# Gated delta attention and a two-layer MLP on one core: chunk 2's normalised rows turned by VectorE and transfers instead of TensorE, with a new order of steps

## The chip, the cores and the metric

The kernel runs on one core of one Trainium2 chip. The metric is device time in microseconds (us); lower is better. TensorE is called PE, VectorE DVE, ScalarE ACT, GpSimd POOL and the engine that issues most transfers SP, as in the profile.

## What is computed

A delta-rule attention runs over 768 positions for 4 batches of 8 heads of width 48, and its output, 768 rows of 384 numbers per batch, goes through a block with layer norm, two matrix products and a residual:

```python
k_n = k / (np.linalg.norm(k, axis=-1, keepdims=True) + 1e-06)
for t in range(S):
    y[:, :, t] = np.einsum('bhd,bhde->bhe', q[:, :, t], state)
    v_old = np.einsum('bhde,bhd->bhe', state, kt)
    state = state + bt[:, :, :, None] * np.einsum('bhd,bhe->bhde', kt, vt - v_old)
...
x = y.transpose(0, 2, 1, 3).reshape(B, S, H * D)
xn = (x - mu) / np.sqrt(var + 1e-06) * g_ln
return x + np.maximum(xn @ w_ch1, 0.0) @ w_ch2
```

All numbers are float32. `w_ch1` is 384 x 1536, `w_ch2` 1536 x 384.

## The kernel before

The 768 positions are cut into 12 chunks of 64 (`C`, `NCH`). A chunk holds the 64 positions of all 32 pairs of batch and head, and gives 256 rows of x (`TOK`), in two groups of 128 (`g`). For each chunk the kernel does the following.

- Keys and queries are brought in with the head's width on the partitions (`first_kt` by PE transposes in the first chunks, `turned`, L753, by DVE from blocks that transfers laid out). `gram` (L790) multiplies keys by keys, `queries` (L799) queries by keys; both run on PE at L775.
- The triangular system of a chunk is inverted. Chunk 0 does it on PE, DVE and ACT in rounds of products called E and Z (`first_inverse`, L648; products at L722 and L741, DVE at L687 and L731, ACT at L681). From chunk 1 on, 32-row blocks are inverted row by row on DVE (`rows_inverse`, L826; L860 and L867), two chunks at a time from chunk 2 on: blocks come by eight transfers `gb` (L833), results go through DRAM (`xd`, L871) and come back by transfers `xt` (L873). `join` (L883) makes 64-row inverses of the blocks: a DVE transpose L888, 64 small matmuls L898, ACT L910, 64 small matmuls L904, ACT L916.
- `recur` (L971) carries the state: products of keys and of queries with the state (L983), the solution u (L1017, copied by ACT at L1019), the state's update (L1034, added by DVE at L1044), and y (L1024). Chunk 0 has its own u (L1000, DVE L1005).
- ACT evicts y as x (L1062) and makes the layer norm (`ln_act`, L939 to L969; DVE takes a reciprocal at L967).
- The normalised rows have to be turned, so that the 384 columns lie on the partitions (`xnt`). Up to chunk `LNPE` PE does this: three 128x128 transposes per group (L1096), each evicted by ACT with the factor g_ln (L1111). Above `LNPE`, DVE turns 32x32 blocks (L1073, two instructions), one transfer writes them to DRAM (`xld`, L1078), four read them back into place (`xnt`, L1082), and ACT multiplies by g_ln (three instructions, L1088).
- The MLP: chunk 0 in halves (`by_halves`, L1317; L1326 and L1341 on PE), chunks 1 to 3 with plain first products (L1300, 12 groups of 6 matmuls; ACT evicts them with ReLU at L1309), and chunks from `FROM` = 4 on with 15 products for the first layer (`fifteen`, L1172; L1221 on PE, sums on DVE at L1241, ACT at L1237 and L1243, differences on POOL at L1197). The second layer of chunks 1 on takes 7 products where a plain one takes 8 (`seven`, L1402; PE at L1423, differences on POOL at L1410 and L1449, sums on DVE and POOL at L1441). Rows that come by the way through DRAM stand in another order within the chunk; L1177 and L1310 put that right in the access patterns, which read `LNPE`.

The weights are fetched as 32-bit words and converted by ACT, DVE and POOL (`fetch`, `convert`, L507 to L544) while chunks 0 and 1 run.

The code first records every piece of work as a numbered step with its engine, without emitting it (`Line.add`). The text `ORDER` (L59 to L156) lists the step numbers, and `Line.emit` (L187) emits them in that order; `in_this_order` (L26) then keeps each engine, and the queues of transfers, to it. So `ORDER` is the order in each engine's queue. An entry `z` emits a fill, a matmul whose result nobody reads (`zeros`, L1514); other fills are steps (`fill`, L553). Each engine takes its instructions strictly in order: one that waits holds up all behind it. POOL and ACT also issue transfers from their own queues.

PSUM has eight banks: `two` and `by` (two each) serve the attention, `f0` to `f3` mostly the MLP. The turn of chunk 2 uses `by`:

```python
for g in range(2) if c <= LNPE else ():
    tp, bk = (by[:, g], BY[2 * g : 2 * g + 2]) if c else ((two, by)[g][:, 0], (TWO, BY)[g][0:2])
```

Of the kernel before, what the change touches and what calls it, by code (L numbers as in the profile page):

```python
# [63 lines left out]
155 243 148 238 151 236 332 152 225 675 156 z 215 157 240 159 158 214 237 239 160 216 162 161 257 46 241 168 164 166 333 206 165 334 245 207 417 163  # L64
# [136 lines left out]
def kernel(  # L201
# [21 lines left out]
    GH = 2 * H  # L223
    NP = H // 2
    TURNED = 4
    LNPE = 2
    GP = 2 * NP
    FROM, LATER = 4, 6
    TOK = 256
# [1423 lines left out]
```

## Time and profile before

| | |
|---|---|
| time, median of 3 runs | 510.0 us (508.62 to 510.16) |
| time of the profiled execution | 510.58 us |
| its span, first to last instruction | 508.8 us |
| granted PE clock, mean over the span | 0.965 |
| busy: PE, DVE, ACT, POOL | 488.6, 353.8, 249.0, 275.6 us |
| PE turns L1096, all chunks (18 instructions) | 2.2 + 0.9 us |
| DVE turns L1073 (18 instructions) | 10.0 us, 565 ns each |
| ACT L1111 (12 + 3) and L1088 (27) | 3.5 + 0.9 and 12.5 us |
| transfers `xld`, `xnt`: median from issue to landing | 3.3 and 3.2 us |

A span is the time between the first and the last instruction on the core; the device time has some 1.8 us around it. A busy time counts an engine's own instructions. A matmul's weights are loaded by a separate instruction (PEld) that overlaps with PE. In the groups, "out<-in" are the program's names. The clock is the share of full speed that PE was granted: in the first 56 us it changes between 0.5 and 1, then it stays at 1 until the end.

### The profile page before, as it was taken

To read this page: it belongs to the slowest core of one execution; us is meant where nothing else is said; L and a number is where in the kernel's file an instruction comes from. 1 tells how busy PE (TensorE), PEld (TensorE's weight loads), DVE (VectorE), ACT (ScalarE), POOL (GpSimd) and SP (SyncE) were. 2 spreads that over 40 slices of the span, in tenths; PEclk is the share of its full clock that TensorE was granted. 3 is DMA by queue.
4 is the path that set the end of the run, shared out by engine and by line. 5 is a ranking of instruction groups with operands and counts; after the bars stand their busy time and mean duration, and the time that the engine had idled before them with its cause. 6 is when DMAs were issued, how large, how long until landed. Compare 5 with 4: busy or idle time off the path is not lost.

```text
span 508.8 us, 22190 instructions
## 1 busy us (share of the span) xinstructions
PE 488.6 (96%) x9606; PEld 447.6 (88%) x9606; DVE 353.8 (70%) x780; ACT 249.0 (49%) x620; POOL 275.6 (54%) x430
## 2 busy tenths in 40 slices
PE   7778999999899999999999999999999999999996
PEld 3667988788788898899999999999999999999996
DVE  9668987997679648896649898568899328143251
ACT  5758873643544524627435535435563257363230
POOL 5464537264755496438894363492543850645633
PEclk9756799999999999999999999999999999999999
DMA  8988796667656566546834434766154402211101
GB/s 168 293 160 190 249 200 85 98 152 130 90 86 87 187 119 119 65 99 149 194 58 62 94 62 135 150 94 97 50 92 106 111 20 45 60 48 46 24 18 31
DMA packets 196097, 54.99 MB, mean 108 GB/s; under 512 B 186076, under 2 KB 189404, under 8 KB 196000
## 3 DMA queue, kind: packets, MB, share of 16 engines
q1 hardware_dynamic: 189920, 40.58, 41.9%
q10 hardware_dynamic: 3872, 9.83, 6.0%
q0 software_dynamic: 2208, 3.17, 3.8%
q8 instruction: 75, 1.23, 1.0%
q14 instruction: 22, 0.18, 0.1%
HBM read 36.64 MB, written 16.91 MB: 105 GB/s over the span
## 4 chain that ended last, share of the span: by engine, by line
PE 90%; DVE 5%; issue 2%; POOL 1%; DMA 1%; SPq 0%; ACT 0%; DVEq 0%; POOLq 0%; ACTq 0%
PE f L1423 29%; PE f L1221 22%; PE f L1300 9%; PE f L1326 4%; PE f L1341 3%; PE by L983 2%; PE by L1024 2%; PE two L983 2%; PE by L775 2%; PE two L1017 2%; PE two L775 2%; PE two L1034 2%; PE f L775 1%; DMA xt<-xd 1%; PE by L741 1%
## 5 line engine op out<-in xcount | busy, mean ns | idle before, releaser
L1410 POOL TENSOR_TENSOR h_all<-h_all 128x256 f32<-128x256 f32 x123 | 89.9, 742 | 135.1 <-PE f L1423 121.3
L1423 PE MATMUL f<-w_sb,h_all 128*128 128x192 f32 x492 | 109.8, 332 | 1.6 <-DVE rstd L967 1.6
L1423 PEld LDWEIGHTS f<-w_sb,h_all 128*128 128x128 f32 x492 | 81.8, 190 | 3.6 <-issue 1.9
L1423 PE MATMUL f<-words,h_all 128*128 128x192 f32 x396 | 84.5, 330 | 0.3 <-POOL h_all L1410 0.3
L860 DVE TENSOR_TENSOR tmp<-xb,gb 128x87 f32<-128x87 f32 (+21 forms) x186 | 73.7, 396 | 4.9
L867 DVE TENSOR_TENSOR xb<-xb,tmp 128x87 f32<-128x87 f32 (+21 forms) x186 | 73.6, 396 | 4.8
L1241 DVE TENSOR_TENSOR h_all<-h_all,f 128x512 f32<-128x512 f32 x96 | 63.5, 682 | 14.3 <-PE f L1221 13.2
L1423 PEld LDWEIGHTS f<-words,h_all 128*128 128x128 f32 x396 | 66.6, 190 | 1.7 <-POOL h_all L1410 1.0
L1300 PE MATMUL f<-xnt,w_sb 128*128 128x256 f32 x216 | 50.2, 382 | 0.0
L349 POOL DMA_DIRECT2D tb<-in_k_dram x64 | 42.0, 660 | 10.3 <-DVE kt L755 9.4
L1243 ACT ACTIVATE h_all<-h_all 128x512 f32<-128x512 f32 x48 | 28.5, 624 | 34.6 <-DVE h_all L1241 34.3
L1300 PEld LDWEIGHTS f<-xnt,w_sb 128*128 128x128 f32 x216 | 40.2, 190 | 5.3
L1237 ACT COPY h_all<-f 128x512 f32<-128x512 f32 x48 | 26.2, 590 | 34.3 <-PE f L1221 17.4
L1441 DVE TENSOR_TENSOR o<-f,x 128x192 f32<-128x192 f32 x33 | 11.6, 352 | 38.9 <-PE f L1423 22.3
L1221 PE MATMUL f<-words,w_sb 128*128 128x128 f32 x256 | 31.7, 276 | 0.0
L1309 ACT ACTIVATE h_all<-f 128x256 f32<-128x256 f32 x36 | 13.3, 382 | 35.1 <-PE f L1300 34.9
L1221 PEld LDWEIGHTS f<-words,w_sb 128*128 128x128 f32 x256 | 30.0, 192 | 0.2
L1221 PE MATMUL f<-xnt,w_sb 128*128 128x128 f32 x192 | 25.4, 276 | 0.0
L542 POOL TENSOR_TENSOR w_sb<-words 128x768 uint32<-128x768 uint32 (+1 forms) x11 | 15.0, 1365 | 17.7 <-DVE words L529 13.3
L1221 PEld LDWEIGHTS f<-xnt,w_sb 128*128 128x128 f32 x192 | 23.7, 192 | 0.1
L1326 PEld LDWEIGHTS f<-xnt,w_sb 128*128 128x128 f32 x144 | 19.2, 200 | 3.3 <-issue 0.2
L1088 ACT ACTIVATE xnt<-xnt,g_sb 128x256 f32<-128x256 f32 x27 | 12.5, 498 | 19.2 <-DMA xnt<-xld 19.1
(246 smaller groups left out, 958.4 us busy)
## 6 DMA issues: line engine op xcount, KB each, us to landing
words<-in_moe_w_ch_dram ACTq DMA_DIRECT2D x10, 768.0 KB, 5.2
gd<-gsb SPq DMA_DIRECT2D x11, 512.0 KB, 3.6
v<-in_v_dram SPq DMA_DIRECT2D x24, 192.0 KB, 4.3
kr<-in_k_dram SPq DMA_DIRECT2D x46, 96.0 KB, 3.6
out_dram<-o SPq DMA_DIRECT2D x44, 96.0 KB, 2.8
xld<-xlt SPq DMA_DIRECT2D x9, 384.0 KB, 3.3
xnt<-xld SPq DMA_DIRECT2D x36, 96.0 KB, 3.2
gb<-gd SPq DMA_DIRECT2D x44, 64.0 KB, 3.0
```

Of the source, the lines that this page charges most:

```text
L349: add(eng, cost, lambda: QUEUE[eng].dma_start(out=out_, in_=in_), r, w, bulk=n * ns / 16e3, **kw)
L775: nc.tensor.matmul(pair[hp][half(e ^ (hp & n)), (g * NP + j) * C : (g * NP + j + 1) * C], kt[drows(hp), l], rt[drows(hp), i],)
L860: lambda j=j, n=n, w=w, t=t: nc.vector.tensor_tensor(out=t, in0=xv[:, 0:n, j : j + 1].to_broadcast([np_, n, w]), in1=gv[:, j : j + 1, j + ...
L867: "DVE", dve(n * w), lambda t=t, rest=rest: nc.vector.tensor_tensor(out=rest, in0=rest, in1=t, op=ALU.subtract),
L1221: nc.tensor.matmul(wide(p[:, 128 * n : 128 * n + 128]), w[n // 2][:, n % 2 * 128 : n % 2 * 128 + 128], r, start=start and n == 0, stop=Tru ...
L1237: add("ACT", act(512), lambda: nc.scalar.copy(o, p), pk, ok)
L1241: add("DVE", dve(512), lambda: nc.vector.tensor_tensor(out=o, in0=o, in1=p, op=op), pk, ok)
L1243: add("ACT", act(512), lambda: nc.scalar.activation(o, o, ACTF.Relu), [], ok)
L1300: nc.tensor.matmul(p[:, 0:TOK], w1_sb[:, t, f * 128 : (f + 1) * 128], xnt[:, t], start=(t == 0), stop=(t == KC - 1))
L1326: nc.tensor.matmul(p[:, 0:128], w1_sb[:, t, f * 128 : (f + 1) * 128], xnt[:, t, cols], start=(t == 0), stop=(t == KC - 1))
L1410: add(eng, cost, lambda: e.tensor_tensor(out=out_, in0=x, in1=y, op=op), r, w, port=2 if eng == "Pool" else 1, pr=-2)
L1423: lambda f=f, t=start and f == 0: nc.tensor.matmul(p[:, 0:D2], lhs(f), rhs[:, f], start=t, stop=(f == F2 - 1), skip_group_check=True),
```

## The change

`LNPE` goes from 2 to 1, so that chunk 2 takes the way of chunks 3 on. Eight steps of chunk 2 (two PE turns of three transposes each, six ACT evictions) give way to ten (two DVE transposes, one transfer to DRAM, four back, three ACT products); all later steps are renumbered by two. `ORDER` is written anew over its whole length, for all engines, with two entries `z` in place of one. Nothing else is changed.

```diff
 ORDER = """
-1 9 49 50 8 63 52 51 10 5 250 54 71 11 56 0 6 14 7 12 47 62 53 48 23 13 72 55 36 18 64 42 26 37 61 27 58 60 77 81 15 28 17 32 331 43 73 88 29 40 65 79
...
 """
@@
     TURNED = 4
-    LNPE = 2
+    LNPE = 1
     GP = 2 * NP
```

The numbers of `ORDER` are left out above but for its first line before. The new order, in the program's names, as far as the steps below speak of it:

- Fills: one of the two stands after an L775 of chunk 0's inverse rounds, ahead of an L741; the other after chunk 0's first L1024, ahead of a gram L775 of chunk 2. Before, the one `z` stands after the first L722.
- ACT's first L426 and L596 stand ahead of L439, so that the built program holds two loads of an activation table in place of one, the second ahead of the first L596. POOL's memset L1539 stands behind the start.
- On DVE, chunk 0's L1005 stands behind an L731 that it was ahead of.
- Between chunk 2's L1024 and chunk 3's L898, PE has three pairs of L1423, where it had 12 pairs, the L1034 and the six turns.
- Between chunk 2's L1024 and chunk 2's first L1300, PE has 29 pairs of L1423, L898, L904, L1034, two L983, L775 and L1017.
- The `xld` transfer of chunk 2 and its four `xnt` stand next to each other on SP, with nothing between.

More of the change, by code (lines that the diff above doesn't have):

```diff
@@ L59 @@
 ORDER = """
[4 rows of a table removed]
-155 243 148 238 151 236 332 152 225 675 156 z 215 157 240 159 158 214 237 239 160 216 162 161 257 46 241 168 164 166 333 206 165 334 245 207 417 163
[88 rows of a table removed]
[3 rows of a table added]
+132 57 139 131 204 z 140 213 38 134 129 133 251 223 135 144 137 222 675 136 205 148 252 67 141 235 256 250 142 208 254 143 242 146 253 150 39 145 206
[3 rows of a table added]
+275 190 191 276 384 247 194 277 249 337 195 382 356 200 278 391 232 359 z 202 338 383 203 279 387 385 339 361 363 201 280 679 389 281 282 396 364 357
[85 rows of a table added]
 """
```

182 rows, old and new, of the table ORDER are left out of this document.

## The prediction

> **What bounds the kernel now.** I read the page first, then busy time by stretch, then the chain of waits in order of time, then the timeline around the places that the change touches. The page has TensorE (PE) nearly always at work and on nine tenths of the chain that ended last:
>
> ```profile
> PE 488.6 (96%) x9606; PEld 447.6 (88%) x9606; DVE 353.8 (70%) x780; ACT 249.0 (49%) x620; POOL 275.6 (54%) x430
> PE 90%; DVE 5%; issue 2%; POOL 1%; DMA 1%; SPq 0%; ACT 0%; DVEq 0%; POOLq 0%; ACTq 0%
> ```
>
> The stretches say where PE is not at work (first busy figure after the length):
>
> ```profile
> 0.00:20.00 20.00, 14.10 (x259) 9.31 (x260) 16.35 (x49) 12.09 (x29) 7.50 (x19) 0.89 0.97 219
> 20.00:40.00 20.00, 14.43 (x439) 12.53 (x441) 12.17 (x35) 12.79 (x33) 12.98 (x19) 0.59 0.82 186
> 120.00:140.00 20.00, 18.28 (x349) 16.28 (x342) 11.88 (x23) 9.70 (x30) 13.95 (x21) 1.00 0.74 98
> 140.00:160.00 20.00, 19.19 (x511) 16.73 (x512) 17.09 (x37) 7.44 (x21) 12.99 (x21) 1.00 0.44 74
> 160.00:480.00 320.00, 320.00 (x6285) 304.63 (x6284) 213.12 (x447) 153.86 (x375) 180.27 (x292) 1.00 0.46 92
> ```
>
> So there are three regimes. Up to about 55 us chunk 0's inverse is a chain of short PE, DVE and ACT steps, at a granted clock of 0.59 in the second row. Between 120 and 160 PE idles 1.72 + 0.81 = 2.53 us. From 160 to 480 it idles not at all: there a new order can win only by less PE work, and it can lose by any wait. Around the edit the chain (start, duration) reads
>
> ```profile
> 30.98 1.15 PE f L1515 x2
> ...
> 78.80 1.08 PE two L983 x64
> 79.87 0.93 PE by L983 x64
> ...
> 102.06 0.65 PE by L1096 x6
> ...
> 120.23 0.52 PE f L1423 x2
> ...
> 123.35 0.34 PE f L1423 x2
> ...
> 141.60 0.81 PE by L1096 x6
> ...
> 143.02 0.81 issue
> ...
> 150.92 2.59 PE f L1300 x12
> ```
>
> and the timeline (start, duration, engine, line; idle before in brackets)
>
> ```profile
> 2.25 1.28 ACT L439 ACT_TABLE_LOAD   x1 [2.25 <-issue]
> ...
> 134.87 0.49 ACT L1062 ACTIVATE x<-by 128x384 f32<-128x384 f32 x1 [1.78 <-PE by L1024]
> 135.79 0.71 DVE L888 STREAM_TRANSPOSE xnj<-xt 128x512 f32<-128x512 f32 x1 [2.63 <-DMA xt<-xd]
> 139.81 1.17 ACT L969 ACTIVATE xln<-xln,rstd 128x384 f32<-128x384 f32 x2 [0.98 <-DVE rstd L967]
> 139.85 0.89 PE L1423 MATMUL f<-w_sb,h_all 128*128 128x192 f32 x4 [1.60 <-DVE rstd L967]
> ...
> 216.66 1.03 DVE L1073 STREAM_TRANSPOSE xlt<-xln 128x384 f32<-128x384 f32 x2
> 222.12 3.48 SPq L349 DMA_DIRECT2D xnt<-xld  x4
> 227.93 1.31 ACT L1088 ACTIVATE xnt<-xnt,g_sb 128x256 f32<-128x256 f32 x3 [7.28 <-DMA xnt<-xld]
> ```
>
> Chunk 2's six turns are at 141.60; its first L1300 runs at 150.92, so nothing waited for them. PE's 1.60 us at 139.85 is DVE's doing: DVE stood 2.63 us at L888 for chunk 3's xt transfers, and the sums L1441 that free PE's banks stood behind it. The 0.81 us "issue" gap at 143.02, like those in the first 37 us (1.10, 1.60, 0.85 and 1.53 us), falls on every 256th PE instruction: an instruction fetch, which the change does not alter.
>
> **The change part by part.** All is summed against the profiled execution: span 508.8 us, its own time 510.58, that is 1.8 us around the span and 0.6 above the median of 510.0. I add the sum to the median.
>
> *Turns taken from PE.* Six L1096 go: 0.65 us where they follow other full-size matmuls (102.06), so −0.65. The ACT work falls from six L1111 (371 ns) to three L1088 (498 ns), 0.7 us on an engine 49% busy: nothing.
>
> *Changes of kind on PE.* A group of 64 small matmuls costs 1.08 us behind a full-size one and 0.93 behind another small group (78.80, 79.87); a full-size pair costs 0.52 behind a small group and 0.34 otherwise (120.23, 123.35). One excursion to small groups and back thus costs 0.15 + 0.18 = 0.33 us. Counted in both orders from chunk 1's L983 on, there are 64 such excursions before and 62 after: −0.7 (0 to −1.4, as two more are saved earlier, at half clock and among waits).
>
> *The new way of chunk 2's x.* Two L1073 (0.565 us each) join DVE, one xld and four xnt transfers SP. SP stands idle from 136.3 to 141.7 us, and in the new order nothing stands between these five: free for others. But the way is longer. From L1062 (134.87) to the end of L969 (140.98) it is 6.1 us, 0.98 of it a wait for DVE; from chunk 4's rows, L1073 at 216.66 to the end of L1088 at 229.24, another 12.6 (the xnt transfers issue 4.4 us after xld, and L1088 starts 5.8 after that). Together 17.7 to 18.7. In the new order PE has, between chunk 2's L1024 and its first L1300: 29 pairs of L1423 (0.325 each, 9.4), L898 and L904 (0.68 each), L1034 (0.86), L983 twice (1.08 each), L775 and L1017 (0.93 each) and three returns (0.19 each), together 16.3. So L1300 waits 1.4 to 2.4 us, and all of PE behind it. I take +1.9 (0 if PE is late there for another reason).
>
> *PE's wait for DVE at 139.85.* In the new order chunk 3's xt transfers stand some two SP issues (0.6 us each) further forward, but between chunk 2's L1024 and chunk 3's L898 PE has 9 L1423 pairs, the L1034 and the six turns fewer (2.9 + 0.86 + 0.81 = 4.6 us), and L888 still blocks DVE ahead of the sums. Between 0 and −1.6; I take −0.6, as the wait is likely met in another place.
>
> *The start.* The program now has two fills (L1515) where it had one. The row is 1.15 us; the second stands after chunk 0's first L1024, ahead of a gram that needs two L573 copies (0.58 each) held behind an L681, so part of it covers a wait: 0 to +1.15, taken +0.6. DVE's L1005 now stands behind an L731 whose product comes after L1000 on PE, not before it: +0.67 + 0.43, less the 0.83 of the last L741, now done ahead: +0.3. And the dummy square root L439, which loaded the square-root table at 2.25 us while ACT waited for data, is moved behind L596, so that the built program has a second table load just ahead of the first L596. POOL's memset L1539 (0.97 us at 2.19, during which DVE's L395 took 1.47 us in place of 0.18) is moved back as well. DVE is then up to 1.2 us sooner with L595, but the load starts only after the second square (about 7.9 us) and takes 1.28, so L596 comes at about 9.2, where it was (9.23). I take 0 (−1.2 to +1.3).
>
> The Trainium skill (ScalarE: Activation LUTs, What ACT_TABLE_LOAD costs) adds a drain of about 1.38 us to each load of another table set. The one load of the trace shows none (the next ACTIVATE starts 1.30 us after it), but nothing was ahead of it; by the page the sum would be 1.4 higher, an estimate.
>
> *160 to 480 us.* No idle to win. If the new order waits as much there as the old one does from 120 to 160, it loses 2.5; if it is as dense, 0. Margins between a PE product and the next use of its bank look alike in both orders; I take +1.0.
>
> Sum: −0.65 − 0.7 + 1.9 − 0.6 + 0.6 + 0.3 + 0 + 1.0 = +1.85, so 511.9 us: a small loss.
>
> **The rivals.** *Faster: the waits that the old order has are gone and the new one is hidden.* If PE comes to L1300 later than its data (any wait of 1.9 us behind L1024, for example at L898 for xt, does that), the term +1.9 falls; if the 1.6 us at 139.85 go wholly and the long stretch stays dense, what is left is −0.65 − 0.7 − 1.6 + 0.9 = −2.05: 507.9. For it: five SP issues and L1073 stand where both queues are free. Against: the way from L1024 has no slack worked out above. It decides once L1300 of chunk 2 waits under 0.5 us.
>
> *Faster: the clock rises one window earlier.* The granted clock changes at 42.8, 46.2 and 56.4, in steps of 3.41 us, and is 0.50 from 46.2 to 56.4 although PE is busy 3.40 of 3.40 us from 49.6 to 53.0, mostly with the small L775. A full-size fill in that window may lift the clock at 53.0. Six L1326 took 1.62 us at half clock and 0.67 later; 3.4 us of such work would take 1.6 to 2.0 less: 511.9 − 1.8 = 510.1, no change. The Trainium skill (TensorE: Matmul & The Clock Gate, What's actually happening) has the clock doubled after one busy window of about 3.4 us; the row from 49.6 to 53.0 does not agree, unless small matmuls count less.
>
> *Slower by more: the first 55 us stretch.* The chain there alternates engines, so one step out of place on DVE is met in full. Five rounds of E and Z products in two halves: if each half-round waits for one DVE L687 or L731 more (0.4 us), it is 10 × 0.4 = 4.0 on top: 515.9. For it: the new order puts a fill between L775 and the next L741 (1.15) and lets half 1 overtake half 0. Against: DVE's work ahead of L1005 is the same but for one L529 (0.35).
>
> *The change does not do what it says:* excluded; L1096 of chunk 2 is gone from the program.
>
> **How the numbers follow.** What a measurement here tells from no change is about 0.3%, 1.5 us. Forecast (+0.5 to +4, its own range 510.5 to 514): 0.42. Waits gone (about 507.9, down to 505.5): 0.28. Clock lifted (about 510.1): 0.16. Long start (about 515.9): 0.14. Faster by over 0.3% takes the second and a little of the third, 0.30; within 0.3% takes most of the third and the lower part of the forecast, 0.21; slower the rest, 0.49. The range leaves out a tenth on each side: below, some of the second case (506.3); above, half of the fourth (516).
>
> **What would show it.** Right: an idle of 1.4 to 2.4 us on PE before chunk 2's first L1300, released by ACT L1088; no L1096 after 110 us; a second ACT_TABLE_LOAD at about 8 us; two L1515 groups; L1326 starting 0.5 to 1.5 us after 54.46. Wrong: L1300 of chunk 2 without a wait, or idle time on PE between 160 and 480 beyond 2.5 us, or a start that differs by more than 2 us either way, since that is the part with the least support.

## The result, and the profile after

| | before | after |
|---|---|---|
| median (lowest to highest of 5 runs) | 509.5 us (507.28 to 510.16) | 515.51 us (514.48 to 516.58) |
| ratio to before, 95% interval | | 1.0141 [1.0111, 1.0171] |
| profiled execution, span | 510.58, 508.8 us | 515.51, 513.3 us |
| PE busy, and idle in the span | 488.55, 20.3 us | 488.2, 25.1 us |

The new order is slower by 7.2 us by the ratio (1.0141 of 508.7); the two profiled executions, which the rest of this section compares, differ by 4.9. The forecast was 511.9, a loss of 1.9: the sign and the range held, the size did not. 0.1% is 0.5 us in all that follows.

The first part of the page of the new kernel (busy time, share, instructions) and its shares of the chain that ended last:

```profile
PE 488.2 (95%) x9602; PEld 446.6 (87%) x9602; DVE 348.7 (68%) x782; ACT 249.3 (49%) x618; POOL 274.5 (53%) x430
PE 82%; DVE 5%; ACT 4%; DMA 3%; issue 2%; SPq 2%; POOL 1%; ACTq 0%; POOLq 0%; DVEq 0%
```

PE does as much as before; the whole difference of the spans is time in which it stands. The chain now has 5% of transfers and SP's queue, and PE 8% less of it. The stretches say where (first busy figure after the length is PE's, clock third from the end):

```profile
0.00:20.00 20.00, 13.39 (x260) 9.12 (x261) 13.25 (x50) 13.09 (x29) 6.97 (x21) 0.90 0.94 210
20.00:40.00 20.00, 15.06 (x462) 12.77 (x460) 13.44 (x36) 14.30 (x36) 13.36 (x16) 0.68 1.01 214
40.00:60.00 20.00, 15.65 (x438) 13.71 (x439) 16.69 (x47) 14.38 (x32) 9.34 (x10) 0.66 0.88 222
60.00:80.00 20.00, 18.40 (x244) 15.92 (x243) 14.46 (x39) 13.37 (x37) 10.21 (x11) 1.00 0.72 170
100.00:120.00 20.00, 18.74 (x323) 15.04 (x322) 18.72 (x46) 8.40 (x25) 7.73 (x12) 1.00 0.67 154
140.00:160.00 20.00, 18.65 (x480) 17.21 (x482) 16.52 (x33) 7.36 (x20) 9.58 (x15) 0.91 0.42 81
160.00:480.00 320.00, 319.04 (x6181) 302.05 (x6172) 213.72 (x449) 153.15 (x375) 177.88 (x289) 1.00 0.47 95
```

Idle time of PE, before and after: 13.1 and 15.9 us up to 60; 0.1 and 1.7 from 60 to 110; 2.5 and 2.6 from 110 to 160; 0 and 1.0 from 160 to 480; 4.5 and 3.9 behind. The differences make +4.8; the spans differ by +4.5, as PE is busy 0.3 less. The timeline (start, duration, engine, line; idle before in brackets, with what ended it) names the waits:

```profile
7.94 1.28 ACT L596 ACT_TABLE_LOAD   x1
9.24 0.21 ACT L596 ACTIVATE knrm<-ksum 128x8 f32<-128x8 f32 x1
...
13.87 0.69 PE L722 MATMUL two<-qt,gsb 64*64 64x64 f32 x32 [2.73 <-DVE qt L710]
...
31.82 1.08 PE L722 MATMUL by<-qt,gsb 64*64 64x32 f32 x32 [2.42 <-ACT xt L681]
...
41.26 0.67 PE L722 MATMUL two<-qt,gsb 64*64 64x32 f32 x32 [1.32 <-DVE qt L687]
...
43.93 1.08 PE L741 MATMUL f<-xt,pt 64*64 64x32 f32 x32 [1.50 <-DVE pt L731]
45.42 1.65 PE L1000 MATMUL two<-v,xt 64*64 64x48 f32 x32 [0.41 <-ACT xt L681]
...
47.83 0.87 PE L722 MATMUL by<-qt,gsb 64*64 64x32 f32 x25 [0.54 <-issue]
49.33 1.08 PE L741 MATMUL by<-xt,pt 64*64 64x32 f32 x32 [0.63 <-DVE pt L731]
50.20 1.08 PE L1024 MATMUL two<-u,pt 64*64 64x48 f32 x32
51.21 1.22 PE L1515 MATMUL f<-ident 128*128 128x256 f32 x2
...
56.82 0.91 PE L1326 MATMUL f<-xnt,w_sb 128*128 128x128 f32 x6
...
64.84 0.27 PE L775 MATMUL f<-kt 48*64 48x64 f32 x2 [1.60 <-issue]
...
117.37 4.15 PE L1300 MATMUL f<-xnt,w_sb 128*128 128x256 f32 x18 [1.26 <-DVE o L1350]
...
144.74 1.15 PE L983 MATMUL two<-s_all,kt 48*64 48x48 f32 x64
145.71 1.05 PE L775 MATMUL by<-qt,kt 48*64 48x64 f32 x57
148.11 0.34 PE L775 MATMUL by<-qt,kt 48*64 48x64 f32 x7 [1.35 <-issue]
148.38 0.81 PE L904 MATMUL f<-xt,es 32*32 32x32 f32 x64
149.12 1.01 PE L1423 MATMUL f<-w_sb,h_all 128*128 128x192 f32 x2
...
152.40 1.30 ACT L1088 ACTIVATE xnt<-xnt,g_sb 128x256 f32<-128x256 f32 x3 [1.66 <-DMA xnt<-xld]
155.84 2.86 PE L1300 MATMUL f<-xnt,w_sb 128*128 128x256 f32 x12
```

In the start, PE's gaps that end in an instruction fetch ("issue") are 1.7 us up to 58, where the old kernel had 5.1; its waits for other engines and for transfers are 14.2 where they were 8.0. Of the 1.7 us of idle time from 60 to 110, 1.60 are one fetch, at 64.84. At 117 a bank waits for the sum L1350, which stands on DVE behind all of a row inverse. At 146.8 a fetch takes 1.35 us in the middle of small matmuls. And chunk 2's L1300 at 155.84 does not wait at all: L1088 ended at 153.70. Three stretches of the clock's 3.41 us show why PE got there so late (same columns as above):

```profile
142.12:145.53 3.41, 3.41 (x69) 3.11 (x71) 3.34 (x9) 0.88 (x3) 2.63 (x4) 1.00 0.32 120
145.53:148.94 3.41, 2.06 (x153) 1.85 (x144) 2.62 (x7) 0.00 (x0) 0.78 (x2) 1.00 0.38 75
148.94:152.35 3.41, 3.41 (x32) 3.35 (x20) 3.05 (x6) 1.46 (x4) 0.00 (x0) 0.50 0.65 104
```

The stretch with the fetch in it is followed by one at half clock, in which ten L1423 matmuls cost twice as much: 1.35 + 1.7 = 3.0 us in this execution.

### The profile page after: what moved, and what is told of

Read it like the earlier page. It is cut to its first block, busy times and chain, and to the rows that moved or that the text cites. A ratio compares the mean times of both kernels' runs of the same rounds, so it can differ in the third digit from the quotient of the medians.

```text
span 513.3 us, 22186 instructions
## 1 busy us (share of the span) xinstructions
PE 488.2 (95%) x9602; PEld 446.6 (87%) x9602; DVE 348.7 (68%) x782; ACT 249.3 (49%) x618; POOL 274.5 (53%) x430
## 4 chain that ended last, share of the span: by engine, by line
PE 82%; DVE 5%; ACT 4%; DMA 3%; issue 2%; SPq 2%; POOL 1%; ACTq 0%; POOLq 0%; DVEq 0%
PE f L1423 28%; PE f L1221 21%; PE f L1300 8%; PE f L1326 3%; PE by L1024 2%; PE by L983 2%; PE two L1017 2%; PE f L1341 2%; PE two L983 2%; PE by L775 2%; SPq L349 2%; DVE xb L867 2%; PE two L1034 1%; PE two L775 1%; DVE tmp L860 1%
## 5 line engine op out<-in xcount | busy, mean ns | idle before, releaser
L1423 PE MATMUL f<-w_sb,h_all 128*128 128x192 f32 x492 | 110.2, 334 | 0.0
L1423 PE MATMUL f<-words,h_all 128*128 128x192 f32 x396 | 85.7, 330 | 0.1
L1423 PEld LDWEIGHTS f<-w_sb,h_all 128*128 128x128 f32 x492 | 82.9, 192 | 1.7 <-POOL h_all L1410 0.2
L860 DVE TENSOR_TENSOR tmp<-xb,gb 128x87 f32<-128x87 f32 (+21 forms) x186 | 74.9, 403 | 5.0
L867 DVE TENSOR_TENSOR xb<-xb,tmp 128x87 f32<-128x87 f32 (+21 forms) x186 | 71.3, 383 | 4.7
L1241 DVE TENSOR_TENSOR h_all<-h_all,f 128x512 f32<-128x512 f32 x96 | 64.2, 683 | 15.1 <-PE f L1221 10.8
L1423 PEld LDWEIGHTS f<-words,h_all 128*128 128x128 f32 x396 | 66.6, 190 | 1.8 <-POOL h_all L1410 0.4
L1300 PE MATMUL f<-xnt,w_sb 128*128 128x256 f32 x216 | 50.6, 383 | 1.7 <-DVE o L1350 1.3
L1300 PEld LDWEIGHTS f<-xnt,w_sb 128*128 128x128 f32 x216 | 40.1, 190 | 8.6 <-DVE o L1350 1.7
L1441 DVE TENSOR_TENSOR o<-f,x 128x192 f32<-128x192 f32 x33 | 11.5, 352 | 41.1 <-PE f L1423 28.8
L1221 PE MATMUL f<-words,w_sb 128*128 128x128 f32 x256 | 32.8, 277 | 0.0
L542 POOL TENSOR_TENSOR w_sb<-words 128x768 uint32<-128x768 uint32 (+1 forms) x11 | 15.2, 1385 | 17.4 <-DVE words L529 8.8
L1221 PEld LDWEIGHTS f<-xnt,w_sb 128*128 128x128 f32 x192 | 23.6, 192 | 0.2
L1088 ACT ACTIVATE xnt<-xnt,g_sb 128x256 f32<-128x256 f32 x30 | 13.7, 500 | 18.6 <-DMA xnt<-xld 18.6
L1019 ACT COPY u<-two 128x768 f32<-128x768 f32 x11 | 8.8, 799 | 28.2 <-PE two L1017 28.2
```

The source lines that it names most:

```text
L860: lambda j=j, n=n, w=w, t=t: nc.vector.tensor_tensor(out=t, in0=xv[:, 0:n, j : j + 1].to_broadcast([np_, n, w]), in1=gv[:, j : j + 1, j + ...
L867: "DVE", dve(n * w), lambda t=t, rest=rest: nc.vector.tensor_tensor(out=rest, in0=rest, in1=t, op=ALU.subtract),
L1221: nc.tensor.matmul(wide(p[:, 128 * n : 128 * n + 128]), w[n // 2][:, n % 2 * 128 : n % 2 * 128 + 128], r, start=start and n == 0, stop=Tru ...
L1241: add("DVE", dve(512), lambda: nc.vector.tensor_tensor(out=o, in0=o, in1=p, op=op), pk, ok)
L1300: nc.tensor.matmul(p[:, 0:TOK], w1_sb[:, t, f * 128 : (f + 1) * 128], xnt[:, t], start=(t == 0), stop=(t == KC - 1))
L1423: lambda f=f, t=start and f == 0: nc.tensor.matmul(p[:, 0:D2], lhs(f), rhs[:, f], start=t, stop=(f == F2 - 1), skip_group_check=True),
```

## The experiments

Each was timed in five rounds beside the old kernel, whose medians in the five sessions were 507.7 to 509.1 us. The ratio is to that.

| | what | median us | ratio [95%] |
|---|---|---|---|
| e1_way_alone | old order, new way | 514.03 | 1.0109 [1.0087, 1.0130] |
| e2_order_alone | new order, old way | 518.42 | 1.0174 [1.0137, 1.0212] |
| e3_old_start | new, old order to 72 us | 511.48 | 1.0054 [1.0033, 1.0074] |
| e4_new_start | old, new order to 72 us | 512.89 | 1.0083 [1.0052, 1.0113] |
| e5_bank | new, L1350 sooner | 515.30 | 1.0129 [1.0096, 1.0163] |
| e6_pool | new, two L542 moved | 515.11 | 1.0131 [1.0092, 1.0171] |
| e7_fetch | new, PE 64 places on | 529.33 | 1.0366 [1.0309, 1.0423] |
| e8_cover | e1 with the wait filled | 513.48 | 1.0087 [1.0056, 1.0118] |
| e9_old_to_36 | new, old order to 36 us | 517.00 | 1.0145 [1.0107, 1.0182] |
| e10_old_to_49 | new, old order to 49 us | 512.35 | 1.0073 [1.0046, 1.0100] |
| e11_sum_sooner | old, one sum L1441 sooner | 509.17 | 0.9999 [0.9978, 1.0020] |
| e12_spread | new, small groups spread | 514.61 | 1.0114 [1.0084, 1.0145] |
| e13_mid_old | new, old order 36 to 49 us | 515.27 | 1.0133 [1.0096, 1.0171] |
| e14_e5_first | new, last L722 first | 515.86 | 1.0149 [1.0117, 1.0181] |
| e15_no_fill | new without second fill | 516.03 | 1.0161 [1.0127, 1.0195] |
| e16_all | e3, e5 and e12 together | 510.61 | 1.0050 [1.0031, 1.0070] |
| e17_old_sp | new, SP's start old | 512.26 | 1.0102 [1.0068, 1.0136] |
| e18_old_engines | new, engines' start old | 513.09 | 1.0100 [1.0065, 1.0135] |

### The way and the order apart

Numbers of `ORDER` are the new kernel's, in e2 the old one's.

```diff
 e1
-    LNPE = 2
+    LNPE = 1
...
-943 840 720
+943 840 847 720
...
+846 848 849 850 851 852 853 722
...
+948 734 854 855 856 1008
 e2
-    LNPE = 1
+    LNPE = 2
...
+919 847 848 849 850 851 852 853 854 581
```

Expected of e1:

> The old order; only chunk 2's turn takes the new way (L1073 behind L969, xld and xnt at once, L1088 ahead of chunk 2's first L1300). Theory A (the loss of the new kernel lies in its order: its first 57 us, a bank wait at 117, an instruction fetch at 147 and the clock window behind it): the six turns save 0.65 us and L1300 waits for the way. In the new kernel L1088 ended 17.4 us after L1024; here L1024 ends at 134.8 and L1300 would come at 150.1, so it waits 2 to 3.5 us: 1.5 to 3 us over before. Theory B (the new way itself, its transfers and DVE turns, makes the loss): 5 us or more over before. Theory C (the way costs nothing, all is order): before or up to 0.7 us under it.

Expected of e2:

> The new order; chunk 2's x is turned by PE as before (the turns stand where L1073 stood). Theory A: the loss stays, and the turns add 0.65 us and a change of kind on PE: 5 to 8 us over before, 0 to 1.5 over the new kernel; the fetch gap at 147 may move by 12 instructions but stays in the run of small matmuls. Theory B: back to before within 1.5 us.

e1 came out at +5.5 us, B's number, but the trace gives A's mechanism with a price that A did not have. The timeline of e1, then two of its stretches:

```profile
152.25 5.49 PE L1300 MATMUL f<-xnt,w_sb 128*128 128x256 f32 x12 [2.80 <-ACT xnt L1088]
```

```profile
148.15:151.56 3.41, 1.30 (x57) 0.95 (x48) 3.24 (x8) 0.89 (x3) 1.37 (x3) 1.00 0.63 114
151.56:154.97 3.41, 2.72 (x6) 2.19 (x7) 2.88 (x5) 1.31 (x3) 0.00 (x0) 0.50 0.66 93
```

The wait is 2.80 us, inside the 2 to 3.5 expected. The clock then stood at 0.50 for two windows of 3.41 us: the twelve L1300 took 5.49 us where the old kernel has 2.59 to 2.75. 2.80 + 2.8 - 0.65 = 5.0 is most of the 5.5. e2 says that the new way is not what costs in the new kernel: with PE's turns back in the new order it was no faster (+8.9 us over before; its interval overlaps the new kernel's). In the old order the way costs 5.5, so the two prices do not add up to the new kernel's 7.2. e8 tested the price of the wait:

```diff
-948 734 854 855 856 1008
+948 734 854 855 856 y 1008
...
+    def other():
+        for _ in range(5):
+            nc.tensor.matmul(by[:, 0, 0:256], ident, ident[:, 0:1].to_broadcast([128, 256]))
```

Expected of e8:

> The kernel of e1_way_alone, with five full-size matmuls (128x256) whose result nobody reads in the place where PE waited 2.80 us for L1088, ahead of chunk 2's first L1300. PE does 2.9 us more work and waits not at all. Theory A (the idle time lowered the clock from 151.6 to 158.4): no half clock there, 2.5 to 3.5 us under e1_way_alone, about 2.2 over before. Rival (the clock fell for another reason): e1_way_alone within 0.5 us.

In its trace the wait is filled and the window from 149.80 is followed by full clock (timeline, then stretches):

```profile
151.13 2.34 PE L1519 MATMUL by<-ident 128*128 128x256 f32 x10
153.47 2.86 PE L1300 MATMUL f<-xnt,w_sb 128*128 128x256 f32 x12
```

```profile
143.00:146.41 3.41, 3.41 (x12) 3.41 (x12) 3.25 (x9) 1.54 (x5) 2.29 (x4) 0.50 0.66 177
149.80:153.20 3.40, 3.40 (x76) 2.98 (x72) 3.23 (x8) 1.31 (x4) 1.23 (x2) 1.00 0.70 120
```

So useless full-size work costs PE nothing there, and the twelve L1300 take 2.86 us. But the medians differ by 0.6 us only (1.1 by the ratios), not by 2.5 to 3.5: this execution lost a window at 143 instead, behind a fetch gap of 1.43 us that e1's trace also has (1.33) without the loss. That the wait lowers the clock is shown in one trace of each; how often it does so is not.

### The start

e3 and e4 exchange the first 495 steps of the two orders; e9, e10 and e13 do it for steps 1 to 235, 1 to 305 and 236 to 305; e17 and e18 for SP's steps alone and for those of PE, DVE, ACT and POOL alone. The first numbers of the order, against the new kernel:

```diff
 e3 e9 e10
-8 5 52 51 4 9 62 71 50 49 10 63 11
+1 9 49 50 8 63 52 51 10 5 250 54 71
 e13
-173 259 421 381 180
+173 259 421 216 381 177
 e17
-8 5 52 51 4 9 62 71 50 49 10 63 11
+8 5 52 49 4 9 62 71 51 50 10 63 54
 e18
-8 5 52 51 4 9 62 71 50 49 10 63 11
+1 9 50 51 8 63 52 10 5 49 250 71 11
```

Expected of e3:

> The steps that the new order has up to about 72 us (495 of them) stand in the old order, all later ones in the new. Theory A: the first L1326 comes some 2.4 us sooner, the rest as in the new kernel: 2 to 4 us under the new kernel, 2 to 4 over before. A rival, D (the start is nothing, since what is late there is met by waits later): the new kernel within 1 us.

Expected of e4:

> The counterpart: the first 495 steps stand in the new order, all later ones in the old, and chunk 2 is turned by PE. Theory A: 2 to 4 us over before, and with the old start's saving it adds up to the whole difference. D: before within 1 us.

Both as A had it: the old start takes back 0.87%, 4.4 us, and the new start alone costs 0.83%, 4.2 us. Start (4.2) and rest (e3's 2.7) nearly make up the 7.2. In the traces the first L1024 of chunk 1 comes at 94.5 us in the old kernel, at 92.7 to 95.0 in all kernels with the old order up to 49 us or further, and at 95.2 to 98.9 in all with the new one or a mixture of the two in time.

The traces also say where in the start the time goes. Six kernels have the old order up to 72 us (the old kernel, e1, e3, e8, e11, e16) and six the new one (the new kernel, e2, e4, e5, e7, e12). Chunk 0's first L1000 starts at 45.0 to 46.9 us (mean 45.8) with the old order and at 45.4 to 48.6 (47.2) with the new one: the two overlap. From there to the first L1326 it takes 7.8 to 8.9 us (8.3) with the old order and 10.8 to 12.5 (11.4) with the new one. So of the 4.6 us that lie between the means at L1326, 1.5 come ahead of L1000 and 3.1 behind it. There the new order puts the last L722 behind L1000 and the fill behind L1024. The two profiled executions have it too; the new kernel is 0.95 us sooner at L1000 and 2.4 later at L1326. The old kernel's timeline, for the rows of the new one above:

```profile
46.37 1.65 PE L1000 MATMUL two<-v,xt 64*64 64x48 f32 x32
...
48.67 1.10 PE L1024 MATMUL two<-u,pt 64*64 64x48 f32 x32 [0.65 <-DVE u L1005]
...
54.46 2.52 PE L1326 MATMUL f<-xnt,w_sb 128*128 128x128 f32 x12
```

Expected of e6:

> The new kernel, with POOL's two L542 at 37.8 us moved, one ahead of L847, one behind two later transfers of POOL's queue. In the new kernel DVE's L850 starts at 37.73, while these two run, and takes 2.79 us; in the old one 1.21 with nothing on POOL. Theory E (DVE waits for POOL there, and the start loses by it): L850 takes 1.2 us, L687 and L731 behind it come 1.3 to 1.6 us sooner, the first L1024 too: 1 to 1.6 us under the new kernel. Rival: the start loses by the order on PE behind it (L1000 ahead of the last L722, a fill) alone: the new kernel within 0.4 us.

```diff
-335 262 181 182 185
+335 216 262 181 182 185
...
-192 228 179
+192 179
...
+676 228 272
```

E is not borne out. L850 did take 1.22 us instead of 2.79, but the new kernel's time stayed: the median is 0.4 under the new kernel's. The interval would still hide the 1 to 1.6 us expected, and in the profiled execution the L722 that mattered waited 2.65 us for a fetch (timeline of e6):

```profile
39.00 1.22 DVE L850 TENSOR_TENSOR gb<-gb,db_b 64x1024 f32<-64x1024 f32 x1
...
50.28 0.87 PE L722 MATMUL by<-qt,gsb 64*64 64x32 f32 x25 [2.65 <-issue]
```

Expected of e9:

> As e3_old_start, but only the first 235 steps (PE to about 36 us: the first three rounds of chunk 0's inverse) stand in the old order, the rest in the new. e3 took back about 4 us. Theory F (the loss lies behind 36 us: L850 beside POOL, the last two rounds with L1000 ahead of the last L722, the fill and L1024): 0 to 1.2 us under the new kernel. Rival G (it lies in the first rounds, with their wait of 2.42 us at 31.8, the table load and the first fill): 2.5 to 4 us under the new kernel.

Expected of e10:

> The same with 305 steps (PE to about 49 us, all five rounds and the first L1000) in the old order; what follows, the last L741 ahead of L1024 and the fill behind it among them, in the new. Theory F: 2 to 3 us under the new kernel, e3's remainder of 1 to 2 us being the fill (1.2 us at half clock) and the order behind it. Rival G: the same as e9_old_to_36 within 0.7 us, and about 1 over e3_old_start.

Expected of e13:

> The new kernel with only its steps 236 to 305 (PE from about 36 to 49 us: the last two rounds of chunk 0's inverse and its first L1000) in the old order. Theory F (the loss of the start lies there): 2.5 to 4 us under the new kernel, as with e10_old_to_49. Rival H (it takes the old first rounds as well, since the two halves run apart from then on): under 1 us.

Expected of e14:

> The new kernel with five steps moved: the last L722 ahead of L1000 on PE, as in the old order, and what feeds it, the L687 of its half ahead of an L731 on DVE and its two L681 ahead of a weight conversion L524 on ACT. Theory F1 (in the new order that L722 comes last before the L731 that L1005 waits for, so that its own lateness and the instruction fetch that falls into it are met in full): the first L1024 1.5 to 2.5 us sooner, 1.5 to 2.5 us under the new kernel. Rival F2 (it is L850 and the rest of DVE's order in that stretch): under 0.7 us.

```diff
-423 193 189
+423 187 193 189
...
-196 246 271
+196 190 191 246 271
...
-274 355 275
+274 194 355 275
```

Expected of e15:

> The new kernel without its second fill (L1515 behind the first L1024; 1.22 us at half clock, which nothing reads). Theory: the gram L775 behind it comes 0.5 to 1.2 us sooner: 0.4 to 1.2 us under the new kernel. Rival (the fill's full-size work keeps the granted clock up, or L775 waits for L573 anyway): the new kernel within 0.4 us, or slower by a clock window's 0.8.

```diff
-232 359 z 202
+232 359 202
```

e10 recovers 3.5 us, e9 and e13 nothing, though together they are e10. So theory F, one bad stretch, is not borne out, nor is G; mixing the two orders in time makes waits of its own (in e9's trace PE stands 2.43 us at 37.93 for chunk 1's keys, whose transfers the old order issues later). e13's trace does have the shorter way from L1000 to L1326 (9.6 us), but its ratio is only 0.08%, 0.4 us, under the new kernel's. e14 and e15 move nothing measurable. e14's trace is no clean test, as the fetch that fell into the last L722 before now fell into L1000, so that L1024 came at 50.19 as in the new kernel (timeline of e14):

```profile
48.62 0.89 PE L1000 MATMUL two<-v,xt 64*64 64x48 f32 x24 [2.12 <-issue]
```

So the stretch is found, but no move in it is shown to be the cause. The chain of waits of the new kernel (start, duration) gives another candidate: it runs through transfers where the old one has PE, DVE and ACT:

```profile
16.20 0.98 ACT gsb L796 x2
...
17.20 6.37 DMA gd<-gsb
...
30.07 2.63 SPq L349
...
32.74 5.01 DMA tb<-in_k_dram
37.75 0.56 DVE gb L850
```

Expected of e17:

> The new kernel; of its first 495 steps only those on SP's queue of transfers stand in the old order, PE, DVE, ACT and POOL in the new. Theory J (the new start is late because of its transfers: in its chain of waits a gd transfer and SP's queue take 17.2 to 32.7 us, where the old chain has PE, DVE and ACT): 2.5 to 4 us under the new kernel. Theory K (the order on the engines): the new kernel within 1 us.

Expected of e18:

> The counterpart: of the first 495 steps those on PE, DVE, ACT and POOL stand in the old order, SP's queue in the new. J: the new kernel within 1 us. K: 2.5 to 4 us under the new kernel, as e3_old_start.

Neither J nor K alone: each half takes back about 0.4%, 2 us, of the 4.4. That would be a loss shared by SP's order and the engines', but both intervals overlap the new kernel's, so it is not shown; which transfer or step it is stays open.

### Bank, fetch and sums

Expected of e5:

> The new kernel, with DVE's last L1350 moved ahead of the row products L860/L867 and of the L1398 that it stood behind. The bank is free at about 115.3 instead of 117.3, so PE's wait of 1.26 us at 117 goes; chunk 2's row inverses come 0.6 us later. Theory A: 0.7 to 1.3 us under the new kernel, unless the wait is met again at chunk 2's first L1300. Rival: the wait is only moved: the new kernel within 0.3 us.

```diff
-703 663 881
+703 881
...
+864 662 663 549 550 551
```

The rival is nearer, though the interval does not exclude A: the wait of 1.26 us is gone, but chunk 2's row inverses came later, L898 then waited 0.55 us for L888 at 128.6, and the median fell by 0.2 us, inside the noise.

Expected of e7:

> The new kernel, with 32 matmuls of 32x32 whose result nobody reads put into PE's wait at 116 us, so that all later PE instructions stand 64 places further. The gap of 1.35 us at 147, on a multiple of 256 PE instructions in the middle of small matmuls, then falls elsewhere. Theory A (the gap lowers the granted clock for the window behind it): gap and half clock at 149 are both gone, 3.0 us, of which chunk 2's first L1300 takes back about 0.9 by waiting for L1088: 1.5 to 3 us under the new kernel. Rival (the fetch comes as late wherever the multiple falls): the new kernel within 0.5 us.

```diff
-871 813
+871 y 813
...
+    def other():
+        for k in range(32):
+            i = 32 * (k % 3)
+            nc.tensor.matmul(f_[0][i : i + 32, 480:512], ident[i : i + 32, i : i + 32], ident[i : i + 32, i : i + 32])
```

Both theories fall, and this is the study's largest effect: 64 PE instructions put into idle time cost 11 us by the ratios (1.0366 against 1.0141). The gap did move, to the next small group, and others that no other kernel has came behind it (timeline of e7):

```profile
150.15 0.26 PE L904 MATMUL f<-xt,es 32*32 32x32 f32 x8 [1.71 <-issue]
...
189.71 0.44 PE L898 MATMUL f<-xnj,gsb 32*32 32x32 f32 x28 [1.26 <-issue]
...
221.55 0.34 PE L775 MATMUL by<-qt,kt 48*64 48x64 f32 x5 [2.24 <-issue]
```

Its profiled execution has 8.5 us of such gaps behind 58 us, where the new kernel has 3.0, and was the fastest of its runs at 522.17. Three others took 528.7 to 529.9, at mean clocks of 0.955 to 0.961 against 0.967; with no trace of them, that their remaining 6.5 to 7.7 us are clock is a guess.

Expected of e12:

> The new kernel with five of the L1423 pairs that stand behind L904 at 149 us moved ahead: three between L983 and L775, two between L775 and L904. The 256 PE instructions up to the fetch at 147 then take about 1 us longer, and the clock's window from 145.5 has full-size matmuls in it. Theory A: the gap shrinks from 1.35 us to 0.4 or less and no half clock follows; of the 3.0 us, chunk 2's first L1300 takes back about 0.9 by waiting for L1088: 1.5 to 2.5 us under the new kernel. Rival (the half clock there is rare, and the gap alone counts): 0.3 to 1 us under it.

```diff
-853 972
+853 944 934 945 972
...
-728 583
+728 935 946 583
```

Theory A in the trace: no gap of its own is left at L775, no half clock follows, and from chunk 2's L1024 to its first L1300 it takes 18.4 us instead of 20.7 (timeline of e12):

```profile
153.58 1.30 ACT L1088 ACTIVATE xnt<-xnt,g_sb 128x256 f32<-128x256 f32 x3
...
155.56 0.70 PE L1300 MATMUL f<-xnt,w_sb 128*128 128x256 f32 x2
```

L1088 ended 0.7 us ahead of L1300: the way is hidden. The ratio is 0.27% better than the new kernel's, 1.4 us; the intervals overlap.

Expected of e11:

> The old kernel, with one sum L1441 moved on DVE ahead of L860 and L867 of 60 columns, behind which it stood while PE waited 1.60 us at 139.85 for its bank. Theory A (the wait is that sum's place in DVE's queue): L1441 runs at 138.3 instead of 139.35, PE waits about 0.5 us: 0.8 to 1.2 us under before, if nothing else meets the wait. Rival (L888's wait for xt holds all of DVE, so that another sum is late next): before within 0.4 us.

```diff
-906 718 834 926 719 912
+906 834 926 912
...
-929 920
+929 718 719 920
```

The rival holds: the wait shrank from 1.60 to 1.00 us, its end passed to DVE's L860, and the time stayed (timeline of e11):

```profile
137.70 0.35 DVE L1441 TENSOR_TENSOR o<-f,x 128x192 f32<-128x192 f32 x1
...
138.19 0.89 PE L1423 MATMUL f<-w_sb,h_all 128*128 128x192 f32 x4 [1.00 <-DVE tmp L860]
```

Expected of e16:

> Three repairs of the new kernel together: the old order up to 72 us (e3_old_start), the bank freed sooner (e5_bank) and the small groups spread (e12_spread). If the causes add up: 4.0 + 0.3 + 1.2 = 5.5 us under the new kernel, 510, 1 to 1.5 over before; what then remains is waits of 1.0 us from 160 to 480 and the way's margin. If they do not (a repaired wait is met later): 511 to 512, as e3_old_start.

The three repairs take back 4.6 us by the ratios (0.91%), of the 5.5 expected; e3 alone has 4.4 of them, so bank and fetch add nothing that can be told apart once the start is repaired. e16 is the fastest kernel with the new way, and still 2.5 us slower than the old kernel. No version tried is faster than the old kernel. Of what is left, 1.0 us is PE's idle time from 160 to 480, which every trace with the new order behind 72 us has (0.9 to 1.5, and 6.4 in e7) and none with the old; the rest is open.

## Why the prediction was off, step by step

- *Turns and changes of kind (-0.65, -0.7).* L1096 fell from 3.1 to 2.3 us, as said. The other saving cannot be read off: PE's busy time fell by 0.3 us in all, with 0.7 more of fills and about 1.7 from the half clock at 149 in it, but the clocks of the two starts differ too much to part the rest.
- *The new way (+1.9).* This step failed: L1300 does not wait, in the new kernel or in any of the 13 other traces with the new way in the new order. PE's work in between was priced rightly (16.2 to 17.2 us, 16.3 forecast). The way was not: from the end of L1024 to the end of L1088 it took 15.3 to 17.4 us, where rows of chunk 4 had given 17.7 to 18.7. The xnt transfers issued 2.4 us after xld, for 4.4 forecast, and the wait of 0.98 us for DVE was gone. Besides, the first L1300 needs only the first of the three L1088: in e1 it starts 0.75 us before the last one ends. The fetch gap and the half clock, 3.0 us in the profiled execution, hide the way there, but they are not needed for it: ten of the 14 traces have no half clock there, and L1300 still does not wait.
- *DVE at L888 (-0.6).* The old wait of 1.6 us went wholly. One like it, 1.26 us, came at 117, which the sum did not have: a bank behind a sum that stands behind row products. Freeing either by itself brought nothing measurable (e5, e11).
- *The start (+0.6 + 0.3 + 0).* This is the step that cost most: 0.9 forecast, 4.2 to 4.4 measured (e3, e4). In the traces it is +1.5 ahead of the first L1000, where the sum had nothing, and +3.1 from there to the first L1326, where it had the 0.9 for L1005 and the fill. It was summed from single changes (fill, L1005, table load, memset). e6, e14 and e15 could not show any single change to be worth its share, nor e9 and e13 either part of the stretch. Perhaps half belongs to the order of transfers on SP (e17), which the prediction did not look at in the start; that is not clear of noise. The prediction also held that the change does not alter the instruction fetches. It does: their gaps are 1.7 us up to 58 where they were 5.1, and 1.60 at 64.84 and 1.35 at 148, where the old kernel has one of 0.81 behind 58 us. The table load did what was forecast: L596 at 9.24 (9.2). No drain shows beside it: it began 0.01 us after the ACTIVATE ahead of it ended and lasted 1.28, so that the 1.38 us of the Trainium skill (ScalarE: Activation LUTs, What ACT_TABLE_LOAD costs) are not seen here. A correction to the list of the change above: L1005 stands behind both L731 in either order; what moved is the last L722, on PE, from ahead of L1000 to behind it.
- *160 to 480 us (+1.0).* Measured: 0.43 + 0.29 + 0.24 = 0.96 us of waits. The figure had been chosen between 0 and 2.5 with no row for it, so that its fit is luck.
- *The rivals.* The long start, at 515.9 with 0.14, is nearest to what happened. That it fits to 0.4 us is luck in part, as its sum holds the +1.9 that did not come. It had ten waits of 0.4 us; the profiled execution has three of 1.3 to 2.4 (at 31.82, 41.26 and 43.93), which fewer fetch gaps made up for until L1000, and the time was lost behind that. The waits rival had L1300 right and the sum wrong, since the start took more than that saved. The lifted clock did not come: the clock's window from 50.0 us, with the second fill in it, was fully busy, and the clock rose only at 56.8, where the old kernel's rose at 56.4. The start has one window less at half clock (30.7 us against 34.1), but earlier, from 26 to 29 us, and it bought nothing visible. e11 has the old start's order and 13.7 us less at half clock than the old kernel's profile, and the same median.

## What to carry to other kernels

When a planner rewrites a whole order, look at the part with the least cover first, here a chain of short steps over PE, DVE, ACT and the transfer queues, and compare the two orders there on the queues as well as the engines; pricing its moves one by one gave a fifth of the loss. A latency should be taken from the place where it will stand: the rows of chunk 4 made the way of chunk 2 some 2 us longer than it was. A wait can cost more than its own length: in e1 one of 2.80 us was followed by two windows at half clock, 2.8 us more. And in a stretch of many small matmuls, the position of PE's instructions on the grid of 256 is a variable of its own (e7: 11 us), so before a difference of 1 to 2% between two orders is put down to a step, look where the fetches fall.

## What the hardware showed that was not expected

*Instruction fetch.* In the 20 traces there are 109 PE gaps of over 0.14 us at places 193 + 256k of PE's instructions (weight loads, matmuls and semaphore instructions counted together). Every one ends 1.2 to 1.9 us (median 1.43) after the end of a packet of 16,384 bytes on the instruction queue q8. That packet starts a median of 3.9 us (1.1 to 6.0) after the previous such place in the first 58 us, where the transfer engines are about nine tenths busy, and 2.1 us (0.5 to 4.0) later. With the packet's own 1.1 us that makes, as an estimate, 6.4 us in the first 58 us and 4.6 later from one place to the next: a block of 256 that PE runs in less is not covered. 64 small matmuls, 128 instructions, take 0.7 to 1.1 us. The old kernel lost 5.9 us to it, the new one 4.6, e7 10.1. The Trainium skill (Runtime: NRT & Kernel Launch, Instruction fetch mechanics) has blocks of 16 KiB, 256 instructions, fetched by the sequencer while the one before runs. The trace agrees with that; the page calls the cost "mostly hidden", which holds for full-size matmuls here (one gap of the 109, 0.53 us in e7, stands before an L1423) and not for small ones.

*What holds the clock up.* All 20 traces were cut into the clock's windows of 3.41 us, and PE's time in full-size matmuls (those that use all 128 rows) was taken apart from that in small ones. 62 windows at full clock were followed by half clock. All but one had at most 0.21 of their time in full-size work (the one, e4's from 4.2 us, had 0.40 and idled for the rest); small matmuls filled up to 0.82. 26 other windows with 0.22 or less stayed at full clock, so a low share goes with nearly every fall but does not make one. Idle time alone does not do it: the old kernel's window from 138.4 has 1.5 us of it, 0.33 of full-size work, and kept its clock. Of 203 windows at half clock 62 rose, all at least 0.92 busy. Among the 89 that were at least 0.97 busy, the clock rose behind 37 of 40 with 0.4 or more of full-size work, and behind 24 of 49 with less, once with none at all (e4's from 14.4 us). The Trainium skill (TensorE: Matmul & The Clock Gate, What's actually happening) has one busy window lift the clock. By these rows a busy window is needed but not always enough. More full-size work goes with a rise; what decides the other windows stays open.
